# SyncE's first transfer in a decode kernel: w1 ahead of wq and the first key tile

## Chip, cores and metric

The kernel runs on one core of one Trainium2 chip. The metric is the device time of one execution in microseconds, the median of several runs. A profile is one execution taken by the hardware profiler; its span runs from the first to the last instruction.

## What is computed

A gated mix of one decode step of attention over a cache, and of a dense layer with squared ReLU. There is one token, 32 heads of width 128 with 4096 cached keys and values each, a model width of 512, and a hidden width of 1376. All inputs are bf16. The reference, cut to what matters:

```python
g = sigmoid((x * gate_w).sum(-1))            # x: 1 x 512
q = (x @ wq).reshape(32, 128)                # wq: 512 x 4096
p = softmax(einsum("hd,hkd->hk", q, k_cache) * 128 ** -0.5)
a = einsum("hk,hkd->hd", p, v_cache).reshape(4096) @ wo    # wo: 4096 x 512
r = relu(x @ w1 + b1)                        # w1: 512 x 1376
b = (r * r) @ w2 + b2                        # w2: 1376 x 512
out = g * a + (1 - g) * b
```

(In the reference `r` is written with `where`, and the batch dimensions of size 1 are kept.) Nearly all bytes are the two caches, 32 heads x 4096 x 128 x 2 bytes each, read once.

## The kernel before

The kernel is written engine by engine, with semaphores by hand; nothing reorders the instructions of an engine. Attention is cut into 8 groups of 4 heads (`NQ = 8`). A group's keys are one transfer of 4 MB, into a tile of 128 partitions; each head has 32 of them, and each partition has 128 blocks of one key (`NB = 128`, `D = 128`). The same holds for the values.

The scores of a group are made in three ways at once, by blocks. GpSimd multiplies 68 blocks by q in four pieces (line 312, `pg`), and VectorE sums them up (line 693). VectorE multiplies and sums 28 blocks in two pieces (lines 678 and 687, `pr`). TensorE transposes the remaining 32 blocks (line 427), ScalarE copies them out of PSUM (line 342), and TensorE multiplies them by q (line 441). VectorE then takes the maximum of the group (line 700). TensorE, VectorE and ScalarE turn it into a bias (lines 451, 704, 455, 352), ScalarE takes exponentials (line 359), and TensorE multiplies them by the values (line 470, `pv`), one to two groups behind the scores.

At the end stand the denominators (line 486), the extraction of the heads' rows (line 479), a regrouping (line 538) and the product with wo (lines 548 and 554), with short fill-in matmuls between them (`busy`, line 570). VectorE adds the dense branch and the bias to the result (line 747), and two small transfers write it out.

At the start, before any of this, TensorE spreads x (line 396), waits for wq (semaphore `s_wq`), and projects it in eight steps (line 412). ScalarE and VectorE copy the results to `qb` (lines 334 and 665), and TensorE turns them into columns (line 404). GpSimd's and VectorE's products need `qb` of their group and the key tile; TensorE's transposes come behind the projection in its order.

After the scores of group 0, TensorE has the dense branch: `mlp_h` (lines 501 and 504, which waits for w1 by `s_w1`), `mlp_c` (line 512) after ScalarE's copy of the row (line 379), and `mlp_out` (line 524), which waits for w2 and for VectorE's squared ReLU (lines 709 and 711). Its end raises `s_ml`.

Memory ties the transfers to each other. There are three key slots (`Kt`) and two value slots (`Vt`). The weights borrow them: wq lies in `Vt` slot 1, w1 and w2 lie in `Kt` slot 2, and wo later in `Vt` slot 0. Key tile 2 thus waits for `s_ml`, and value tile 1 waits for the projection and the dense branch (`s_qr`, `s_h`). The last two value tiles go into key slots.

All large transfers are issued by SyncE, on one queue, in this order: wq (line 246, ahead of the engine's block), key tile 0 (line 260 by `load_k`), w1 (277), w2 in six pieces (278, 279, 281), key tile 1, value tile 0, all without a wait; then key tile 2 (after `s_ml`), key tile 3, value tile 1, and from there a key tile and a value tile in turn, as GpSimd, VectorE and TensorE release their slots, and at the end wo in four pieces (line 292). x, gate_w, b1 and b2 are small and are issued by ScalarE (lines 319 to 324). The readers wait each for the semaphore of their own transfer; none of them relies on the order of issue.

Of the kernel before, what the change touches and what calls it, by code (L numbers as in the profile page):

```python
# [5 lines left out]
def bass_gated_mix__gqa_block_cached__dense_activation_squared_relu__decode_kernel(  # L6
# [70 lines left out]
    wq_v = A_wq.rearrange("(p t) n -> p (t n)", t=4)  # L77
    wo_v = A_wo.rearrange("(p t) n -> p (t n)", t=32)
    w1_v = B_w1.rearrange("(p t) n -> p (t n)", t=4)
# [6 lines left out]
    with ctx:  # L86
# [6 lines left out]
        def sem(name):  # L93
            return ctx.enter_context(nc.semaphore(name))
# [4 lines left out]
        wq_f = Vt[:, 1, :]  # L99
# [9 lines left out]
        w1_sb = WM[:, 0:4 * F]  # L109
# [62 lines left out]
        def VT(i):  # L172
            return Vt[:, i % NV, :] if i < NQ - 2 else Kt[:, (i - 1) % NK, :]
# [15 lines left out]
        s_wq = sem("s_wq")  # L189
        s_w1 = sem("s_w1")  # L190
# [52 lines left out]
        s_fin = sem("s_fin")  # L243
        s_out = sem("s_out")

        nc.sync.dma_start(wq_f, wq_v).then_inc(s_wq, 16)

        def on(engine):
            return lambda part: part(engine)

        @on(nc.sync)
        def _(eng):
            def load_k(i):
                if i >= NK:
                    eng.wait_ge(s_t, CB[i - NK + 1])
                    eng.wait_ge(s_mu, XP * (i - NK + 1))
                    eng.wait_ge(s_pm, GP * (i - NK + 1))  # L257
                if i == 2:
                    eng.wait_ge(s_ml, 1)
                eng.dma_start(Kt[:, i % NK, :], k_p[i * 128:(i + 1) * 128, :]).then_inc(s_k[i % NK], 16)  # L260

            def load_v(i):
                if i == 1:
                    eng.wait_ge(s_qr, NQ)
                    eng.wait_ge(s_h, 2)
                if i < NQ - 2:
                    if i >= NV:
                        eng.wait_ge(s_pv, i - NV + 1)
                    eng.dma_start(VT(i), v_p[i * 128:(i + 1) * 128, :]).then_inc(s_v[i % NV], 16)
                    return  # L270
                eng.wait_ge(s_t, CB[i])
                eng.wait_ge(s_mu, XP * i)
                eng.wait_ge(s_pm, GP * i)
                eng.dma_start(VT(i), v_p[i * 128:(i + 1) * 128, :]).then_inc(s_vl[i - (NQ - 2)], 16)  # L274

            load_k(0)
            eng.dma_start(w1_sb, w1_v).then_inc(s_w1, 16)
            eng.dma_start(w2a, w2_v).then_inc(s_w2, 16)
            eng.dma_start(w2b, B_w2[F0:F1, :]).then_inc(s_w2, 16)
            for r in range(4):  # L280
                eng.dma_start(WX[r:QX:4, :], w2_x[r:QX:4, :]).then_inc(s_w2, 16)
            load_k(1)
            load_v(0)
            load_k(2)
            for i in range(NQ):
                if i >= 1:
                    load_v(i)
                if i + LAG < NQ:
                    load_k(i + LAG)
            eng.wait_ge(s_pv, NQ - 3)  # L290
            for c in range(NW):
                eng.dma_start(WO[:, TS[c] * DM:TS[c + 1] * DM], wo_v[:, TS[c] * DM:TS[c + 1] * DM])\  # L292
                   .then_inc(s_wo[c], 16)
            eng.wait_ge(s_fin, 1)
            eng.dma_start(out_v[2:4, :], b2w[32:34, :]).then_inc(s_out, 16)
            eng.wait_ge(s_out, 32)
# [479 lines left out]
```

## Time and profile before

| | |
|---|---|
| median of 3 runs | 189.68 us (189.59 to 189.73) |
| the profiled execution, its time | 189.88 us |
| its span | 188.6 us |
| busy: VectorE | 152.8 us (81% of the span) |
| busy: GpSimd | 137.8 us (73%) |
| busy: TensorE matmul | 108.2 us (57%) |
| busy: ScalarE | 69.4 us (37%) |
| read from HBM | 78.32 MB, 415 GB/s over the span |
| SyncE's queue | 97.2% of 16 DMA engines' span |
| mean granted TensorE clock | 0.71 |

Times in the timeline are microseconds from the span's start. A row of a timeline is: start, duration, engine, line, operation, tile written and tile read, how many were merged, and in brackets the idle time before and what ended it. A DMA's issue on SyncE is a row of its own (SPq) and short; its data lands much later, and the trace gives the time from issue to landing. In the slices of the span each digit is a fortieth of it, 4.7 us.

### The profile page before, as it was taken

The numbers are of one execution on the slowest core, as the hardware profiler recorded it, in microseconds if no ns is written. First come the engines' busy times: TensorE is split into PE (matmuls) and PEld (weight loads), VectorE is DVE, ScalarE is ACT, GpSimd is POOL, SyncE is SP. The second block draws the span as 40 slices with busy tenths as digits, with TensorE's granted clock in tenths as the row PEclk, the third lists the DMA queues.
The fourth block names the chain that finished last, engine by engine and source line by source line (L and its number), as shares of the span: only waits on it lengthen the run. The fifth ranks groups of instructions, "written<-read, shape, count | busy, mean of one in ns | idle before, by whom it ended". The sixth has DMA issues, their size and how long they took to land. (4 is left out here: it accounts for less than half of the span.)

```text
span 188.6 us, 2602 instructions
## 1 busy us (share of the span) xinstructions
PE 108.2 (57%) x1071; PEld 64.4 (34%) x1071; DVE 152.8 (81%) x128; ACT 69.4 (37%) x169; POOL 137.8 (73%) x38
## 2 busy tenths in 40 slices
PE   1129877778203837147506481858184748469985
PEld 0013243337103617133404180417141733224334
DVE  5113559999997999999999999999999999991030
ACT  2102485218220829304910572056405551406000
POOL 1000199998996999989998999999899989940000
PEclk9999999765555887657955855555755586655899
DMA  6999899999999999999999999999999999999992
GB/s 223 446 445 438 386 441 441 438 438 424 436 424 431 433 424 428 438 431 424 421 445 424 445 424 428 445 417 431 424 434 431 431 438 438 428 431 400 423 400 102
DMA packets 3416, 78.47 MB, mean 416 GB/s; under 512 B 423, under 2 KB 441, under 8 KB 718
## 3 DMA queue, kind: packets, MB, share of 16 engines
q1 hardware_dynamic: 3388, 78.32, 97.2%
q8 instruction: 8, 0.13, 0.3%
q14 instruction: 2, 0.02, 0.0%
q10 hardware_dynamic: 18, 0.01, 0.0%
HBM read 78.32 MB, written 0.00 MB: 415 GB/s over the span
## 5 line engine op out<-in xcount | busy, mean ns | idle before, releaser
L312 POOL TENSOR_TENSOR pg<-Kt,qb 128x2176 f32<-128x2176 bf16 x32 | 137.1, 4317 | 28.6 <-DMA Kt<-in_A_k_cache_dram 23.3
L693 DVE TENSOR_REDUCE Sb<-pg 128x17 f32<-128x2176 f32 x32 | 77.0, 2405 | 2.0 <-POOL pg L312 2.0
L342 ACT ACTIVATE kT<-T 128x1024 bf16<-128x1024 bf16 x32 | 30.8, 1030 | 16.4 <-PE T L427 16.4
L427 PE MATMUL T<-ident,Kt 128*128 128x128 bf16 x256 | 25.7, 282 | 18.1 <-DMA Kt<-in_A_k_cache_dram 18.1
L678 DVE TENSOR_TENSOR pr<-Kt,pQ 128x1792 f32<-128x1792 bf16 x16 | 32.2, 2011 | 2.0 <-DMA Kt<-in_A_k_cache_dram 1.1
L687 DVE TENSOR_REDUCE Sb<-pr 128x14 f32<-128x1792 f32 x16 | 32.1, 2004 | 0.0
L427 PEld LDWEIGHTS T<-ident,Kt 128*128 128x128 bf16 x256 | 22.5, 131 | 22.7 <-DMA Kt<-in_A_k_cache_dram 21.0
L470 PE MATMUL pO<-Vt,E 128*16 128x512 bf16 x192 | 21.1, 530 | 0.5 <-issue 0.5
L352 ACT ACTIVATE nM<-pM 128x4 f32<-128x4 f32 x8 | 1.4, 174 | 48.5 <-PE pM L455 48.5
L359 ACT ACTIVATE E<-Sb,nM 32x128 bf16<-32x128 f32 x32 | 18.5, 580 | 0.9
L441 PE MATMUL pS<-qc,kT 128*128 128x4 bf16 x256 | 11.7, 168 | 10.1 <-ACT kT L342 9.9
L479 PE MATMUL pX<-pvf,pick 112*32 112x128 f32 x64 | 14.3, 398 | 2.4 <-ACT pvf L365 2.4
L451 PE MATMUL pM<-identf,mp 128*1 128x128 f32 x8 | 2.8, 347 | 20.7 <-DVE mp L700 20.7
L441 PEld LDWEIGHTS pS<-qc,kT 128*128 128x128 bf16 x256 | 10.0, 103 | 12.3 <-ACT kT L342 12.2
L412 PE MATMUL T<-Vt,kT 128*128 128x512 bf16 x32 | 10.5, 474 | 3.5 <-DMA Vt<-in_A_wq_dram 3.5
L479 PEld LDWEIGHTS pX<-pvf,pick 112*32 112x32 f32 x64 | 9.3, 158 | 5.9 <-ACT pvf L365 2.9
L334 ACT ACTIVATE qb<-T 32x128 bf16<-32x128 f32 x20 | 5.4, 269 | 10.3 <-PE T L412 9.9
L470 PEld LDWEIGHTS pO<-Vt,E 128*16 128x16 bf16 x192 | 6.4, 103 | 6.3 <-issue 4.0
L455 PE MATMUL pM<-gm,onesf 1*128 1x4 f32 x16 | 3.9, 308 | 8.1 <-DVE gm L704 8.1
L451 PEld LDWEIGHTS pM<-identf,mp 128*1 128x1 f32 x8 | 0.6, 80 | 22.4 <-DVE mp L700 22.0
L359 ACT ACTIVATION_READ_ACCUMULATOR E<-Sb,nM 32x1 f32 x32 | 8.1, 253 | 0.0
L455 PEld LDWEIGHTS pM<-gm,onesf 1*128 1x128 f32 x16 | 3.1, 244 | 13.4 <-DVE gm L704 13.4
(79 smaller groups left out, 76.0 us busy)
## 6 DMA issues: line engine op xcount, KB each, us to landing
Kt<-in_A_k_cache_dram SPq DMA_DIRECT2D x8, 4096.0 KB, 31.0
Vt<-in_A_v_cache_dram SPq DMA_DIRECT2D x6, 4096.0 KB, 31.3
Kt<-in_A_v_cache_dram SPq DMA_DIRECT2D x2, 4096.0 KB, 31.3
Vt<-in_A_wq_dram SPq DMA_DIRECT2D x1, 4096.0 KB, 12.4
Vt<-in_A_wo_dram SPq DMA_DIRECT2D x1, 2048.0 KB, 31.7
Kt<-in_B_w_dram SPq DMA_DIRECT2D x1, 1376.0 KB, 24.6
Kt<-in_B_w_dram SPq DMA_DIRECT2D x1, 1280.0 KB
Vt<-in_A_wo_dram SPq DMA_DIRECT2D x1, 1152.0 KB, 34.2
```

What stands on the lines that cost most here:

```text
L312: eng.tensor_tensor(pg[:, n % 2, 0:g, :], Kt[:, i % NK, k * g * 128:(k + 1) * g * 128] .rearrange("p (b d) -> p b d", b=g), qb[:, i:i + 1, ...
L342: eng.activation(kT[:, n % NR, :], T[n % NT][:, :].bitcast(bf16), ACT.Copy).then_inc(s_ev, 1)
L359: eng.activation(E[a:b, j % NE, :, h], Sb[a:b, j % NS, :], ACT.Exp, bias=nM[a:b, 4 * j + h:4 * j + h + 1], scale=SCALE, accum_out=RS[a:b, ...
L412: mm = eng.matmul(T[j % NT][:, :], xb[:, t, :], wq_sb[:, t, j * 512:(j + 1) * 512], start=(t == 0), stop=(t == 3))
L427: mm = eng.transpose(T[n % NT][:, :].bitcast(bf16)[:, y * 128:(y + 1) * 128], Kt[:, i % NK, w * 128:(w + 1) * 128], ident[:, :])
L441: mm = eng.matmul(S[:, c * TC + y, :], kT[:, n % NR, y * 128:(y + 1) * 128], qc[:, 4 * i:4 * i + 4], start=True, stop=True)
L455: eng.matmul(MB[:, 4 * i:4 * i + 4], onesf[:, :], gm[:, 4 * i:4 * i + 4], start=True, stop=True) .then_inc(s_mb, 1)
L470: mm = eng.matmul(pO[r:r + 16, :], E[:, i % NE, 4 * y:4 * y + 4, :], VT(i)[:, y * 512:(y + 1) * 512], start=(y < 4), stop=(y >= NG - 4))
L479: mm = eng.matmul(O, pick[0:112, b, 28 - 4 * i:60 - 4 * i], pvf[:, b * 128:(b + 1) * 128], start=False, stop=(i == NQ - 1 and b == 3), ski ...
L678: eng.tensor_tensor(pr[:, 0:x, :], Kt[:, i % NK, a * 128:(a + x) * 128] .rearrange("p (b d) -> p b d", b=x), PQ[:, i % 4:i % 4 + 1, :].bro ...
L687: eng.tensor_reduce(Sb[:, i % NS, a:a + x], pr[:, 0:x, :], AX.X, ALU.add).then_inc(s_sd, 1)
L693: eng.tensor_reduce(Sb[:, i % NS, k * g:(k + 1) * g], pg[:, n % 2, 0:g, :], AX.X, ALU.add)\
```

## The change

SyncE's first three transfers are issued in another order. Before: wq, key tile 0, w1. After: w1, wq, key tile 0. The transfer of w1 takes the place ahead of SyncE's block that wq had; wq becomes the first of the block. The semaphores, the destinations, the sizes and all that follows (w2, key tile 1, value tile 0 and the rest) are as they were. The instructions of the other engines are the same, in the same order.

```diff
-        nc.sync.dma_start(wq_f, wq_v).then_inc(s_wq, 16)
+        nc.sync.dma_start(w1_sb, w1_v).then_inc(s_w1, 16)
...
+            eng.dma_start(wq_f, wq_v).then_inc(s_wq, 16)
             load_k(0)
-            eng.dma_start(w1_sb, w1_v).then_inc(s_w1, 16)
             eng.dma_start(w2a, w2_v).then_inc(s_w2, 16)
             eng.dma_start(w2b, B_w2[F0:F1, :]).then_inc(s_w2, 16)
```

## The prediction

> **What bounds the kernel now.** I read the slices of the span first, then the chain that ended last, then the timeline of each engine at the start, in the middle and at the end.
>
> ```profile
> DVE  5113559999997999999999999999999999991030
> POOL 1000199998996999989998999999899989940000
> DMA  6999899999999999999999999999999999999992
> ```
>
> The reader is to see two things that are full at the same time: the DMA engines from end to end, and VectorE (with GpSimd) from slice 7 or so to slice 36. VectorE's row has one weaker digit in between, the 7 of the 13th slice (56.6 to 61.3 us). That digit is where this change will be decided. In the windows view VectorE is busy 108.79 of the 110.00 us from 59.84 to 169.84, so after that point it has nothing to give back.
>
> The last pieces of the chain that ended last, then TensorE's last pieces in the timeline (start, duration, idle time before in brackets):
>
> ```profile
> 150.53 35.31 DMA Vt<-in_A_wo_dram
> 185.89 1.03 PE pX L554 x28
> 186.94 0.28 DVE b2w L747
> ```
>
> ```profile
> 171.54 1.92 PE L479 MATMUL pX<-pvf,pick 112*32 112x128 f32 x8
> 173.39 2.31 PE L570 MATMUL T<-kT,ident 128*128 128x512 bf16 x5
> 175.63 0.22 PE L486 MATMUL pM<-onec,RS 128*32 128x1 f32 x2
> 175.78 1.25 PE L570 MATMUL T<-kT,ident 128*128 128x512 bf16 x5
> 176.97 1.90 PE L470 MATMUL pO<-Kt,E 128*16 128x512 bf16 x32
> ...
> 184.45 1.18 PE L554 MATMUL pX<-Vt,o2p 128*2 128x128 bf16 x36
> 185.89 1.01 PE L554 MATMUL pX<-Vt,o2p 128*2 128x128 bf16 x28 [0.27 <-DMA Vt<-in_A_wo_dram]
> ```
>
> By name the last transfer of wo ends the kernel, at 185.89. But TensorE waits for it only 0.27 us: the computed tail (the last keys' scores, maximum, exponentials, PV, the wo rows) gets there almost at the same moment. So there are two near-critical chains, the DMA stream and the VectorE chain with its tail, and the second has 0.27 us of slack.
>
> Now the start: issues on SyncE, and the first use of what they bring.
>
> ```profile
> 0.73 0.39 SPq L246 DMA_DIRECT2D Vt<-in_A_wq_dram  x1
> 1.18 0.41 SPq L260 DMA_DIRECT2D Kt<-in_A_k_cache_dram  x1
> 1.64 0.44 SPq L277 DMA_DIRECT2D Kt<-in_B_w_dram  x1
> ```
>
> ```profile
> 22.96 21.53 POOL L312 TENSOR_TENSOR pg<-Kt,qb 128x2176 f32<-128x2176 bf16 x5 [21.50 <-DMA Kt<-in_A_k_cache_dram]
> ...
> 59.89 4.32 POOL L312 TENSOR_TENSOR pg<-Kt,qb 128x2176 f32<-128x2176 bf16 x1 [1.78 <-DMA Kt<-in_A_k_cache_dram]
> ```
>
> ```profile
> 59.84 2.02 DVE L678 TENSOR_TENSOR pr<-Kt,pQ 128x1792 f32<-128x1792 bf16 x1 [1.12 <-DMA Kt<-in_A_k_cache_dram]
> ```
>
> From issue to landing the trace gives 12.4 us for wq (lands at 13.1), 21.7 for key tile 0 (22.9) and 24.6 for w1 (26.2): they land in the order of issue, one after the other. GpSimd starts within 0.1 us of key tile 0's landing, so all the attention work hangs on that landing. Key tile 2 lands at 59.8 (issued at 41.3, 18.5 us); there GpSimd has been idle 1.78 us and VectorE 1.12 us. These are the only cushions after the start.
>
> **The change, part by part.** Nothing is added or removed, the instructions of the four compute engines keep their order; on SyncE one issue moves past two others. All of them are issued without a wait within the first 7 us (w2, key tile 1 and value tile 0 behind them keep their places), so issue costs nothing: the three take 0.39 to 0.44 us each, and the sum is the same before w2.
>
> w1 lands first. Its reader (line 504) starts at 31.2 now, 5 us after the 26.2 at which w1 lands, because TensorE has the scores of tile 0 ahead of it. TensorE's order is unchanged, so an early w1 is worth nothing.
>
> wq lands later by w1's transfer. 1376 KB (1.41 MB) at the slices' 386 to 446 GB/s is 3.65 to 3.16 us; the two landings, 26.2 less 22.9, give 3.3, and I take that: wq at 16.4, key tile 0 at 26.2. w2 and everything behind stays where it is, since the bytes ahead of it are the same. The projection of q (lines 411 to 416 and its copies) moves with wq by 3.3; its first result is copied by 16.3 now, 19.6 then, still 6.6 us before key tile 0, so for GpSimd the keys stay last. VectorE's own copies of q end at 23.28 now, 26.6 then; its product starts right after, and it then waits for GpSimd's first block in any case (1.97 us idle in the trace).
>
> So GpSimd's and VectorE's work on tiles 0 and 1 moves by 3.3 us. Key tile 2's landing does not move unless its issue becomes late: it waits for the dense branch (semaphore s_ml, 41.3), which moves to 44.6. Value tile 0, the last transfer queued before it, lands at 49.8 (6.79 plus 43.0). The queue holds 5.2 us of work, and from the first issue at 0.73 to the first bytes it is about 1 us (windows view: none before 1.0), so the stream has no hole. Cover gone: every us beyond 48.8 would be a us of the end.
>
> At tile 2 the cushions are used up: VectorE, ready at 58.72 now, is ready at 62.0, with the keys already there: 3.3 less 1.12 leaves **2.2 us**. GpSimd keeps 3.3 less 1.78, which is 1.5, so VectorE decides. From there VectorE is full to 169.9 (the 110 us above) and the 2.2 us go through. Later issues of keys and values, released by GpSimd and PV, get up to 3.3 us later, but they land 25 to 34 us after issue and stand behind queued ones: the stream does not notice. The last value tile, issued at 149.2 behind 17 us of queued work (its predecessor lands at 166.6), lands at 176.4 as now.
>
> The tail moves by 2.2: last maximum (line 700) at 172.1 for 169.9, PV of the last group at 179.2 for 177.0, well after its values. TensorE comes to the last wo rows 2.2 us later, its 0.27 us wait vanishes, and the output is **1.9 us** later. Sum: 3.3 - 1.12 - 0.27 = 1.9. The profiled execution has a span of 188.6 and a time of 189.88, 1.3 around it; it would become 190.5 and 191.8. The median of the runs, 189.68, is 0.2 below the profiled one; I forecast 189.68 + 1.9 = **191.6 us**. With the bounds of w1's transfer alone, 3.16 to 3.65, it is 191.4 to 191.9.
>
> What the trace does not show is TensorE's clock in a shifted tail. The windows view has granted clock 0.50 from 172 to 175.5 and 1.00 from 175.6 on. At half clock five fill-in matmuls (line 570) take 2.31 us, at full 1.25, and the ones before line 486 hold up the denominators: the exponentials end at 174.25, line 486 starts at 175.63. The bounds: if the clock is full early, those 1.4 us go and the end is only 0.5 later than now (190.2); if it stays half up to 179.0, some two of the second five matmuls cost double, 0.45 us more (192.1). I take the clock to move with the work, as the middle.
>
> **Rivals.**
>
> (a) No change, 189.7. The stream is full, its bytes are the same, and it ends at 185.9 by name. For it: the chain that ended last is DMA. Against it: the computed tail may move by only 0.27 us, so key tile 0 would have to land less than about 1.8 us later (1.12 + 0.27 + 0.38 of what can't be told apart). That takes w1 to overlap with wq, or the order of landing not to follow the order of issue; the three landings speak against both.
>
> (b) Faster. From 20 to 25 us the stream moves 384 GB/s against 431 later, 0.55 us lost just where keys end and w1 begins. If that seam costs nothing at the head, where the queue is only filling, the stream ends at 185.3 and the kernel at 189.1. It decides only if key tile 0 lands less than 0.8 us later than now (1.12 + 0.27 - 0.55), against 3.3 by w1's size.
>
> (c) Slower by less: full clock early in the tail, +0.5 to +1.4, 190.2 to 191.1. For it: the granted clock changes at 32.2, 35.6, 39.0, 62.9 and 175.6, in multiples of 3.4 us, on a grid whose place in another run is open. Against: TensorE stands idle 2 us longer just ahead of the last maximum.
>
> (d) Slower by a little more: full clock late. If the grid lies as here, the steps at 175.6 and 179.0 are the candidates. In the trace TensorE is busy all of the 3.4 us before 175.6; in the shifted tail it is so only from 173.7 (line 479 at 171.5, plus 2.2), so the step at 179.0 is the likely one: 192.1 by the bound above. [...]
>
> (e) Slower by more: TensorE at half clock also in the dense branch. Its hidden row (line 504) runs a quarter at full clock now; wholly at half, it ends 1.2 us later (8 matmuls of 512 columns at the 0.46 us of line 570's half-clock row and 4 of 352 columns at 0.32 are 5.0 us against 3.79), VectorE's step at line 709, which has 0.5 us to spare (37.85 to 38.36), stalls 0.7, and the sum is 2.6 or, with a late clock, up to 3.5: 192.3 to 193.2.
>
> **How the numbers follow.** Forecast, from 191.2 to 191.9: 0.42. (d), 191.9 to 192.3: 0.24. (c) 0.16, (e) 0.08, (a) 0.06, (b) 0.04. Range 190.3 to 192.8: all of the forecast and of (d), nearly all of (c), half of (e), about 0.85. 0.2% (0.38 us) is about what a measurement here tells from no change; faster is (b), 0.04; same is (a), 0.06; slower is the rest, 0.90.
>
> **What would show it.** Key tile 0's landing and GpSimd's first product at 26.2 for 22.96. VectorE's 1.12 us idle for key tile 2 gone, GpSimd's 1.78 too, and line 678 of tile 2 at 62.0; last maximum near 172.1; no wait for wo before the last matmuls of line 554, while wo still lands near 185.9; span 190.5. It is wrong if GpSimd starts before 24.7, if VectorE waits for keys at tile 2 again, or if the DMA digits show a hole near 50 us.

## The result, and the profile after

The changed kernel took 192.54 us in the median (six runs, 191.12 to 193.03), the kernel before 189.70 (six runs, 189.59 to 189.91). The ratio is 1.0133, with a 95% interval of 1.0091 to 1.0175: slower by 1.7 to 3.3 us. The profiled execution took 192.19 with a span of 190.9, that is 2.3 more than the profiled one of before in both.

The issues of SyncE, from the timeline of the changed kernel (start, duration, line, tile written and read):

```profile
0.73 0.39 SPq L246 DMA_DIRECT2D Kt<-in_B_w_dram  x1
1.18 0.41 SPq L276 DMA_DIRECT2D Vt<-in_A_wq_dram  x1
1.63 0.47 SPq L260 DMA_DIRECT2D Kt<-in_A_k_cache_dram  x1
...
44.42 0.80 SPq L260 DMA_DIRECT2D Kt<-in_A_k_cache_dram  x2
```

From issue to landing they take 5.8, 15.1 and 24.3 us: w1 lands at 6.5, wq at 16.3, key tile 0 at 25.9, again one after the other. GpSimd and VectorE in the timeline:

```profile
26.03 21.38 POOL L312 TENSOR_TENSOR pg<-Kt,qb 128x2176 f32<-128x2176 bf16 x5 [24.56 <-DMA Kt<-in_A_k_cache_dram]
48.35 17.10 POOL L312 TENSOR_TENSOR pg<-Kt,qb 128x2176 f32<-128x2176 bf16 x4 [0.94 <-DVE Sb L693]
```

```profile
59.79 2.00 DVE L687 TENSOR_REDUCE Sb<-pr 128x14 f32<-128x1792 f32 x1
62.34 2.02 DVE L678 TENSOR_TENSOR pr<-Kt,pQ 128x1792 f32<-128x1792 bf16 x1 [0.56 <-DVE Sb L687]
...
172.43 0.29 DVE L700 TENSOR_REDUCE mp<-Sb 128x1 f32<-128x128 f32 x1
```

GpSimd starts 3.07 us later (22.96 before). Its wait for key tile 2 is gone: from 48.35 it runs through. VectorE's first product of tile 2 comes at 62.34 for 59.84, 2.50 later, and no longer waits for a DMA; but there are 0.56 us of idle time that the profile can pin on nothing except the sum before it. The last maximum is 2.50 late too: nothing in the 110 us between gives a microsecond back. Its row before:

```profile
169.93 0.29 DVE L700 TENSOR_REDUCE mp<-Sb 128x1 f32<-128x128 f32 x1
```

The chain that ended last, in order of time, has changed its nature. Before, the last transfer of wo stood in it; now it is computed from the last maximum to the end, and no transfer stands in it:

```profile
172.43 0.30 DVE mp L700
...
174.10 1.84 PE pX L479 x8
175.95 0.33 issue
176.28 1.91 PE T L570 x4
178.19 0.20 PE pM L486 x2
178.39 1.43 PE T L570 x5
179.82 1.86 PE pO L470 x32
...
187.41 1.80 PE pX L554 x64
189.22 0.02 issue
189.24 0.28 DVE b2w L747
```

The last wo matmuls (line 554) run as one block of 64 here; before, they stood in two, with a wait for wo between. Their end moves from 186.90 to 189.20, by 2.30. TensorE's timeline and granted clock in this stretch (windows view: stretch, length, busy time of the engines, then granted clock, DMA share and GB/s):

```profile
167.16 2.65 PE L470 MATMUL pO<-Kt,E 128*16 128x512 bf16 x29
172.78 0.37 PE L451 MATMUL pM<-identf,mp 128*1 128x128 f32 x1 [2.97 <-DVE mp L700]
...
179.75 1.90 PE L470 MATMUL pO<-Kt,E 128*16 128x512 bf16 x32
```

```profile
170.00:172.00 2.00, 0.00 (x0) 0.00 (x0) 2.00 (x2) 0.47 (x1) 0.00 (x0) 1.00 0.99 426
172.00:174.00 2.00, 0.85 (x3) 0.56 (x3) 0.91 (x3) 0.00 (x0) 0.00 (x0) 0.51 0.89 385
174.00:176.00 2.00, 1.95 (x9) 1.38 (x11) 0.00 (x0) 1.77 (x7) 0.00 (x0) 0.50 0.94 401
176.00:178.80 2.80, 2.52 (x8) 0.85 (x9) 0.15 (x1) 0.70 (x4) 0.00 (x0) 0.50 1.01 430
178.90:182.00 3.10, 3.10 (x39) 1.11 (x37) 0.29 (x1) 0.00 (x0) 0.00 (x0) 1.00 0.97 406
```

This is the second thing to read. PV of group 6 still hangs on its values and is over at 169.8, while the last maximum has slipped to 172.4, so TensorE stands idle for 2.97 us. The clock, granted in full from 168.6 on and through that idle time (1.00), drops to half at 172.0, just where the tail begins (0.50 from 172.1 to 178.8), and is full again only from 178.9. The same stretch in the kernel before, timeline and windows:

```profile
166.76 3.59 PE L470 MATMUL pO<-Kt,E 128*16 128x512 bf16 x32 [2.08 <-issue]
170.28 0.37 PE L451 MATMUL pM<-identf,mp 128*1 128x128 f32 x1
```

```profile
172.00:174.00 2.00, 2.00 (x9) 1.14 (x8) 0.00 (x0) 1.91 (x8) 0.00 (x0) 0.50 1.03 442
174.00:175.50 1.50, 1.50 (x4) 0.30 (x2) 0.00 (x0) 0.24 (x2) 0.00 (x0) 0.50 0.87 371
175.60:177.00 1.40, 1.40 (x12) 0.58 (x15) 0.15 (x1) 0.00 (x0) 0.00 (x0) 1.00 1.02 433
```

There TensorE went from this PV to the last maximum without idle time, and yet its clock was half as well, 0.50 from 161.9 until 175.6. The clock turned full 3.3 us later, the work came 2.5 us later.

### The profile page after: what moved, and what is told of

Same layout as the page of the kernel before. It is cut to its first block, busy times and chain, and to the rows that moved or that the text cites. A ratio compares the mean times of both kernels' runs of the same rounds, so it can differ in the third digit from the quotient of the medians.

```text
span 190.9 us, 2600 instructions
## 1 busy us (share of the span) xinstructions
PE 108.3 (57%) x1069; PEld 64.9 (34%) x1071; DVE 152.8 (80%) x128; ACT 69.4 (36%) x169; POOL 137.7 (72%) x38
## 5 line engine op out<-in xcount | busy, mean ns | idle before, releaser
L427 PE MATMUL T<-ident,Kt 128*128 128x128 bf16 x256 | 24.8, 275 | 8.6 <-DMA Kt<-in_A_k_cache_dram 8.6
L427 PEld LDWEIGHTS T<-ident,Kt 128*128 128x128 bf16 x256 | 21.7, 127 | 13.1 <-DMA Kt<-in_A_k_cache_dram 10.5
L470 PE MATMUL pO<-Vt,E 128*16 128x512 bf16 x192 | 23.9, 582 | 0.0
L665 DVE CAST qb<-T 32x128 bf16<-32x128 f32 x12 | 3.4, 287 | 9.8 <-PE T L412 9.6
L470 PEld LDWEIGHTS pO<-Vt,E 128*16 128x16 bf16 x192 | 7.0, 108 | 6.3 <-issue 4.5
## 6 DMA issues: line engine op xcount, KB each, us to landing
Vt<-in_A_wq_dram SPq DMA_DIRECT2D x1, 4096.0 KB, 15.1
```

Source lines behind the costliest of these rows:

```text
L427: mm = eng.transpose(T[n % NT][:, :].bitcast(bf16)[:, y * 128:(y + 1) * 128], Kt[:, i % NK, w * 128:(w + 1) * 128], ident[:, :])
L470: mm = eng.matmul(pO[r:r + 16, :], E[:, i % NE, 4 * y:4 * y + 4, :], VT(i)[:, y * 512:(y + 1) * 512], start=(y < 4), stop=(y >= NG - 4))
```

## The experiments

Each time stands beside the kernel before on the same chip (medians 189.75 to 189.80).

**e1: only the keys late.** Order wq, w1, key tile 0.

```diff
-            load_k(0)
             eng.dma_start(w1_sb, w1_v).then_inc(s_w1, 16)
+            load_k(0)
```

> Order wq, w1, key tile 0: wq keeps its place, only the keys are late. Theory (the landing of key tile 0 decides, wq's does not): GpSimd starts at 26.0 as with the change, VectorE is 2.5 us late from tile 2 on, 191.1 to 193.0 us as with the change. Rival (the late wq and the late projection cost the time): TensorE's projection starts at 13.2 again and the time is within 0.4 of before, 189.3 to 190.1.

Measured: 191.82 us (191.28 to 193.01). GpSimd's first product in the timeline:

```profile
26.15 21.39 POOL L312 TENSOR_TENSOR pg<-Kt,qb 128x2176 f32<-128x2176 bf16 x5 [24.69 <-DMA Kt<-in_A_k_cache_dram]
```

VectorE starts tile 2 at 62.45. With wq at its old place the time is that of the change, so wq's lateness costs nothing that these runs can show; what counts is w1 ahead of the keys.

**e2: half the bytes.** Two of the four rows per partition of w1 ahead of wq, the others after key tile 0; the dense branch waits for both.

```diff
-        nc.sync.dma_start(w1_sb, w1_v).then_inc(s_w1, 16)
+        nc.sync.dma_start(w1_sb[:, 0:2 * F], w1_v[:, 0:2 * F]).then_inc(s_w1, 16)
...
             load_k(0)
+            eng.dma_start(w1_sb[:, 2 * F:4 * F], w1_v[:, 2 * F:4 * F]).then_inc(s_w1, 16)
```

> Half of w1 (688 KB) ahead of wq, the other half after key tile 0. Theory (delay by bytes, less the cushion at tile 2): key tile 0 lands 1.5 us late, at 24.4; VectorE at tile 2 starts 0.5 to 1.0 us late (1.5 less the 1.12 idle, with or without the 0.4 us gap seen there with the change); 189.9 to 190.6 us. Rival (any transfer ahead of wq costs the same, for instance by the queue's start): 191.1 to 193.0 as with the change.

Measured: 189.53 us, but with runs in two groups: nine from 189.30 to 189.85, three from 190.97 to 191.12. These three have the lowest mean granted clock of the twelve (0.667 to 0.676; the others have 0.691 to 0.728). GpSimd starts at 24.33, 1.37 late, VectorE at tile 2 at 60.63, 0.79 late. The delay goes by bytes (1.37 us for 688 KB, 3.07 for 1376). The median is below what I expected, and the time is the same as before (ratio 1.0008, interval 0.9987 to 1.0028).

**e3: twice the bytes.** The large part of w2 goes ahead of wq too.

```diff
+            eng.dma_start(w2a, w2_v).then_inc(s_w2, 16)
             eng.dma_start(wq_f, wq_v).then_inc(s_wq, 16)
             load_k(0)
-            eng.dma_start(w2a, w2_v).then_inc(s_w2, 16)
```

> w1 and the large part of w2 (1280 KB) ahead of wq. Theory (delay by bytes): key tile 0 lands 6.1 us late, at 29.0; VectorE starts tile 2 5.0 to 5.4 us late and stays so; key tile 2 is issued at 47.4, 2.4 us before the queue runs dry, so no hole; 194.3 to 196.0 us. Rival (the late release of the slot opens a hole in the stream near 50 us): key tile 2 lands over 1 us later than 59.9 and the time is over 196.2. Rival (only TensorE's clock matters): under 194.

Measured: 195.09 us (194.29 to 196.06). GpSimd starts at 29.11 (6.15 late), VectorE at tile 2 at 65.43 (5.59 late): the same sum, 6.15 less 1.12 plus the same 0.56. But one expectation missed. Key tile 2 was issued at 47.50 and landed only at 62.2 (14.7 later), 2.3 later than in the changed kernel (59.9), and the windows view has the hole:

```profile
46.00:48.00 2.00, 2.00 (x17) 0.69 (x12) 1.87 (x2) 0.50 (x1) 2.00 (x2) 0.50 0.73 311
48.00:50.00 2.00, 2.00 (x22) 2.00 (x20) 2.00 (x2) 1.63 (x3) 2.00 (x1) 0.50 0.95 262
```

311 and 262 GB/s where the changed kernel moves 492 and 393, although the last transfer queued before lands at 49.6 in this run as well (6.64 plus 43.0). The hole costs nothing here, because VectorE is later than the stream anyway (65.43 for 62.2).

**e4: TensorE kept busy ahead of the last maximum.** The changed order, with six more fill-in matmuls; their results are read by nobody.

```diff
             pv(NQ - 2, 0, NG)
+            busy(6)
             max_rows(NQ - 1)
```

> The changed kernel with six more fill-in matmuls (line 570's) ahead of the last maximum, where TensorE stands idle 3 us; nothing else is changed. Theory (of the 2.8 us of the change up to 1.9 are TensorE's half clock in the shifted tail): full clock at or before 175.5, line 486 within 0.4 us of the last exponential, 190.3 to 191.4 us and all runs within 1 us. Rival (the tail is late by VectorE alone and the clock is no part of it): 192.2 to 193 with runs between 191 and 193 as with the change.

Measured: 190.26 us, just below what I expected; six of seven runs from 190.22 to 190.38, one at 191.18. TensorE in the timeline, and the granted clock:

```profile
170.75 1.47 PE L570 MATMUL T<-kT,ident 128*128 128x512 bf16 x6
172.85 0.27 PE L451 MATMUL pM<-identf,mp 128*1 128x128 f32 x1 [0.63 <-DVE mp L701]
...
176.65 0.20 PE L486 MATMUL pM<-onec,RS 128*32 128x1 f32 x2 [0.30 <-ACT E L359]
176.78 1.25 PE L570 MATMUL T<-kT,ident 128*128 128x512 bf16 x5
177.97 1.90 PE L470 MATMUL pO<-Kt,E 128*16 128x512 bf16 x32
```

```profile
172.00:174.00 2.00, 1.00 (x6) 0.57 (x6) 0.98 (x3) 0.10 (x1) 0.00 (x0) 1.00 0.86 369
174.00:176.00 2.00, 1.86 (x13) 0.94 (x11) 0.00 (x0) 1.88 (x8) 0.00 (x0) 1.00 0.96 410
```

VectorE is as late as in the changed kernel (tile 2 at 62.42), and yet 1.6 to 2.3 us are gone (against the changed kernel's medians of 191.81 and 192.54). The clock is full all through the tail (1.00 from 172 to 182), the denominators (line 486) come right after the last exponential instead of behind half-clock matmuls, and PV starts at 177.97 for 179.75. The clock turned full at 170.4 (0.89 from 170 to 172, 1.00 behind it), before the six matmuls began; with them it stayed full. In the 3.4 us behind that step TensorE is busy 2.40 us here, and the clock stays at 1.00. In the changed kernel the clock turned full at 168.6, TensorE was busy only 1.19 of the next 3.4 us, and the clock dropped to 0.50. That the work in this stretch decides is not shown by these two cases.

**a2: the changed kernel again.**

> The changed kernel again, beside the next three on one chip. Both theories: 191.0 to 193.1 us, the runs spread over more than 1 us; VectorE's first product of tile 2 starts 0.55 us after the sum before it ends, as in every kernel with late keys so far.

Measured: 191.81 us (191.19 to 192.97), gap 0.55. Its profiled execution was the fastest of the six, 191.19: the clock turns full at about 177.6 there, 1.3 earlier than in the first one, and PV starts at 178.74 for 179.75. The delay of VectorE is the same (last maximum at 172.40).

**e5: the fill-in in the kernel before.** The same line added to the old order.

> The kernel before with the six fill-in matmuls ahead of the last maximum. Theory (before is held by the stream alone, its tail has no clock to gain): line 486 may start up to 1.4 us earlier, TensorE then waits over 1 us for the last transfers of wo, 189.4 to 189.9 us, no change. Rival (the tail in half clock holds the kernel before too): under 189.2.

Measured: 189.73 us (189.59 to 189.89), ratio 1.0000 (0.9991 to 1.0009). The last wo matmuls of TensorE's timeline:

```profile
184.26 1.17 PE L554 MATMUL pX<-Vt,o2p 128*2 128x128 bf16 x36
185.79 1.02 PE L554 MATMUL pX<-Vt,o2p 128*2 128x128 bf16 x28 [0.37 <-DMA Vt<-in_A_wo_dram]
```

No gain, as expected, since wo holds the end. The wait grew only to 0.37 us, not over 1, because PV's last group, at 176.62, comes only 0.35 us earlier. Two things hold it. Its values land at about that time (176.4 in the trace of before). And here, where TensorE had no idle time, the six matmuls themselves delay the last maximum's (line 451):

```profile
170.04 1.47 PE L570 MATMUL T<-kT,ident 128*128 128x512 bf16 x6
171.34 0.27 PE L451 MATMUL pM<-identf,mp 128*1 128x128 f32 x1
```

It starts at 171.34 for 170.28, so that the denominators come 0.49 us earlier (175.14 for 175.63) and not 1.4. The six take 1.47 us, 0.25 each, as line 570's five do in the kernel before at a granted clock of 1.00 (1.25 us; 2.31 at 0.50). So the clock is full from 170.04 at the latest in this run.

**e6: half of w1 first, with the fill-in.**

> Half of w1 first, with the six fill-in matmuls. Theory (the runs of the half near 191 us are half clock after an idle TensorE): all runs within 0.5 us, 189.2 to 189.7 us, TensorE waits for wo. Rival (those runs come from something else): some runs near 191 stay.

Measured: 189.43 us, all eleven runs from 189.29 to 189.73; ratio 0.9982 (0.9974 to 0.9991). The group of runs near 191 us is gone. The fill-in is the only difference from e2, and the three runs of e2 near 191 us had its lowest clock (0.667 to 0.676), so this points to the clock; no trace shows one of those runs. The kernel beats both kernels, by 0.3 us against the kernel before. The block of the last wo matmuls (line 555 in this file) takes 2.25 us instead of the 1.96 of one that need not wait, so wo is only a little late in it. The block ends at 186.52, for 186.90 in the kernel before; why wo lands earlier here is open.

**e7 and e8: VectorE's 0.43 us.** The gap before VectorE's first product of tile 2 is 0.13 at the other tiles and 0.54 to 0.56 in every kernel with late keys so far, at the same place in the program and at different times (60.63 to 65.43). e7 is e4 with eight tiny memsets at the head of VectorE's program, where VectorE is idle; they fill a tile of their own. e8 is the same kernel, timed.

```diff
+            for u in range(8):
+                eng.memset(pad[:, u:u + 1], 0.0).then_inc(s_pad, 1)
             eng.memset(b2w[:, :], 0.0).then_inc(s_wm, 1)
```

> The changed kernel with the fill-in matmuls and eight more tiny memsets at the head of VectorE's program, where it has nothing to do; they write a tile that nobody reads. It asks for the 0.43 us that VectorE stands before its first product of tile 2. Theory (it belongs to a place in VectorE's stream of instructions, so it moves by eight instructions): the gap before that product is 0.13 and a gap of about 0.4 us appears earlier, somewhere in tile 1, or is hidden. Rival (it belongs to tile 2's keys or product): the gap stays at 0.55 at the same product. Time 189.8 to 190.5 us either way.

> The kernel of e7 again, timed in rounds: changed order, fill-in matmuls, eight tiny memsets. Theory (VectorE's 0.43 us belongs to a place in its instructions and the tail follows it): 189.8 to 190.0 us against e4's 190.26. Rival (e7's 189.88 was one lucky run): 190.2 to 190.4.

Measured: 189.88 us in e7's one run, 189.77 in e8 (twelve runs, ten of them up to 190.05, two at 190.32 and 190.69). VectorE in e7's timeline:

```profile
59.78 2.00 DVE L692 TENSOR_REDUCE Sb<-pr 128x14 f32<-128x1792 f32 x1
61.91 2.02 DVE L683 TENSOR_TENSOR pr<-Kt,pQ 128x1792 f32<-128x1792 bf16 x1
```

The sum ends at the same time as in the changed kernel, and the product follows after 0.13 us. The gap does not turn up elsewhere: behind the waits of the start (the last, of 2.29 us, ends at 30.36), no idle time of VectorE before the last maximum is above 0.13. So it belongs to a place in VectorE's instructions, not to tile 2's keys. What happens at that place is not shown. In the kernel before, this place lies in the wait for key tile 2 (1.12 us).

**e9: half of w1, fill-in and memsets.**

> Half of w1 first, fill-in matmuls and the eight memsets. Theory (with half of w1 and the fill-in the stream decides, so VectorE's 0.43 us is worth nothing there): 189.2 to 189.6 us, as e6's 189.43, the gap before VectorE's first product of tile 2 at most 0.13. Rival (VectorE still decides there): 189.0 to 189.1.

Measured: 189.48 us (189.31 to 189.99), gap 0.13. The memsets move VectorE, not the time: with half of w1 the stream decides again.

## Why the prediction was right, and where it was off

**Direction and mechanism: right.** Key tile 0 behind w1, cushions at tile 2, full VectorE, a tail that overtakes the stream: each step is in the trace, and e1, e2 and e3 show that it goes by the bytes ahead of the keys. The rivals "no change" and "faster" needed key tile 0 to land under 1.8 and 0.8 us later; it landed 3.0 later.

**The sum, term by term, against the profiled execution.** The 3.3 us for w1 was 3.07. The 1.12 us of idle time at tile 2 were there, but not all of them could be used: VectorE stands 0.56 us at that product even when it waits for no transfer (0.13, the usual gap, and 0.43 that belong to this place), and the 1.12 us wait for the keys had covered this. So VectorE came 2.50 late, for the 2.2 of the prediction. The cushion at the end, put at 0.27, was 0.49: the block of line 554 took 2.45 us with its wait (184.45 to 186.90) and takes 1.96 without. 3.07 - 1.12 + 0.56 - 0.49 is 2.0, and TensorE's later clock adds 0.28 (PV 2.78 late for VectorE's 2.50): 2.3, which is what the profiled execution lost. The forecast had 1.9. It put the 0.56 at nothing, and it had the transfer 0.23 too long and the last cushion 0.22 too short; that these nearly cancel is luck.

**The clock: the term that was mis-sized.** "I take the clock to move with the work" is the weak step. In the profiled execution it does so but for 0.28; full clock comes at 178.9, as in rival (d), which put the cost at 0.45. In a2's profiled execution the tail gains 0.70 instead (PV 1.77 late, the last maximum 2.47). The median, 192.54, lies 0.35 above the profiled execution, and single runs reach 193.0, beyond the 192.1 that I took as the bound of a late clock: that bound was wrong. The whole spread of 1.9 us comes with one and the same order of instructions. What the clock did in the slowest runs has no trace, but each run's mean granted clock is on record: of the twelve runs of the changed kernel (with a2), the five over 192.8 us have 0.679 to 0.697, the six under 191.9 us have 0.721 to 0.731. The kernel before has 0.674 to 0.746 at nearly one time (189.51 to 190.10), so the clock counts only where the tail ends last.

**What the fill-in takes back.** e4 takes back 1.6 to 2.3 us, most of what the change costs. But this is what a tail in full clock is worth against one in half clock, not what the idle time costs. The kernel before has the same loss: its denominators come 1.38 us behind the last exponential (174.25 to 175.63), and in the changed kernel's profiled execution it is 1.38 us too (176.74 to 178.12). Before, the loss was hidden, because wo ended the kernel; with VectorE 2.5 us late it shows. How much of it the idle time causes is open: in e4, with the fill-in, the clock is 1.00 from 172 on where the changed kernel has 0.50, and the kernel before had 0.50 until 175.6 without idle time.

Where the clock turns full was not the same from run to run: the same kernel turns to full clock at 178.9 in one profiled execution and at 177.6 in another, and with the idle time filled six of e4's seven runs lie within 0.16 us. Rival (d) took the step at 179.0 for the likely one because TensorE was busy all of the 3.4 us before 175.6. That was one step, and the trace has another case: in the kernel before TensorE is busy all of the 3.4 us from 39.0 to 42.4 as well, and the clock stays at 0.50 until 62.9. What decides a step is not shown.

**What the delay alone is worth.** With the fill-in and without VectorE's gap, the changed order takes 189.77 us against 189.80 before (e8; ratio 1.0008, 0.9998 to 1.0018). The last maximum is 2.06 us late in e7's trace of the same kernel (171.99; the matmul behind it starts at 172.34 in both), the tail in full clock takes 1.58 of it back (PV at 177.45, 0.48 late), and the cushion of 0.49 takes the rest. The kernel before with the same fill-in takes 189.73 us (e5), so nothing is left of the delay, and nothing is won.

**The stream: right in result, wrong in reserve.** In the changed kernel key tile 2 was issued at 44.42 and no hole opened (492 and 393 GB/s from 46 to 50). But "every us beyond 48.8" was too generous: in e3 an issue at 47.50 already left one. There 2.1 us ahead of the last landing (49.6 less 47.5) were too few, for the 1 us of the prediction; 5.4 us, in the changed kernel, were enough. What lies between was not measured. Rival (e) did not come: VectorE did not wait for TensorE in the dense branch (line 709 starts at 41.42, right behind the sum before it).

## What to carry to other kernels

When a transfer is put ahead of the one that starts the longest chain, count its bytes as delay of that chain (here 1.37, 3.07 and 6.15 us for 688, 1376 and 2656 KB), then subtract the idle time that the chain has later (here 1.12 less 0.56 at tile 2, and 0.49 at the end). What remained went through to the end here, 2.3 us in the profiled execution with the clock's 0.28, although SyncE's queue had been 97.2% busy before. Where two chains end within half a microsecond of each other, as here, the one that the profile names last is not the only bound. And look at what a delay does to a third engine: here it opened 2.97 us of idle time on TensorE right before the tail, the granted clock dropped there from 1.00 to 0.50, and six useless matmuls in that place, with which it stayed at 1.00, were worth 1.6 to 2.3 us. Part of that gain was no repair: the old tail ran in half clock too, until 175.6, and nobody saw it while a transfer ended last.

## What was not expected of the hardware

Once the computed tail ended last, one program spread over 1.9 us (191.12 to 193.03), with full clock in the tail from 178.9 in one profiled execution and from 177.6 in another. The kernel before, whose end a transfer holds, stays within 0.6 us (189.51 to 190.10 in all runs beside the experiments). VectorE stood 0.43 us longer than usual at one place of its program in six kernels (the changed one, e1 to e4, e6), and eight memsets ahead of it, some 60 us earlier, took that away.
